# Pacing the weight-split loads of an adaLN transformer block by TensorE, storing the split weights one tile later, and the order of added exponential tiles

## The chip, the cores and the metric

The kernel runs on one core of a Trainium2 chip. The metric is the device time of one execution in microseconds, median over runs. TensorE (PE) does the matmuls, VectorE (DVE), ScalarE (ACT) and GpSimd (POOL) the elementwise work, and every DMA of this kernel is issued from one queue, that of SyncE (SP), which issues in its written order: an entry that has to wait holds all behind it.

## The reference

One transformer block on x of 2048 × 576 with 32 heads of 18 and an MLP of 4608, all in float32:

```python
mod = (silu(c) @ w_mod).reshape(1, 6, 1, 576)   # sa, ca, ga, sb, cb, gb
h = layernorm(x) * (1 + ca) + sa
x = x + ga * attention(h, wqkv, wo)             # softmax(q k^T / sqrt(18)) v, then wo
h = layernorm(x) * (1 + cb) + sb
x = x + gb * (silu(h @ w1) @ w2)
```

## The kernel before

Matmul operands are split into a high and a low float32r part, and a product is made of three matmuls (high × high, high × low, low × high). Weights arrive as plain float32. A weight tile is split once, on GpSimd, stored to a scratch tensor in HBM (`w1s`, `w2s`, `wos`), and later loaded from there as a pair, once for each of the four blocks of 512 query rows.

The work runs in stages:

1. A start (to about 155 us of the profile): layer norm, transposes, the first Q and K columns, V.
2. Attention, as a long row of slots: 32 heads in quads of 4, 4 query blocks, 32 slots to each quad and block. A slot holds two score matmuls in one orientation for the row maximum (`psa`, L727, reduced by VectorE at L729), two in the other (`psb`, L777) whose exponential ScalarE writes to a tile `pt` (L779), and the value matmuls (`psv`, L814) follow a few slots behind.
3. Beside the slots runs a *filler*, a list of pieces of other matmul work that a planner mixes in: first the remaining Q and K projections (`psqk`, L569, to about 612 us), then, for each query block that attention has finished, the output projection (`psp`), layer norm, and the MLP (`ps`, L483 and L477, one pair of w1 tiles after another, four w2 tiles at a time). The last block's MLP has no attention beside it (from about 2200 us).

TensorE's order is that of the program, set by the planner's modelled times. The other engines' order, SP's among them, is set when the kernel is built by a scheduler that simulates it: an instruction is placed when its inputs and buffers are free in that simulation, so a load that depends on nothing but a free buffer is placed early, whatever the place in the program it was asked for.

Names that the change and the prediction touch:

- `early` (L633) and `weights` (L636): split one weight tile of the filler's first stage. The list `splits` holds 36 tiles of w1 and 5 of wo; `add_qk` (L608) puts one after the second and one after the fourth quarter of each Q/K block of 14 matmuls. `weights` loads the raw tile in two halves (`raw`, L644, a ring of 3), makes the high part (L647) and the low part (L648) on GpSimd, and stores the pair (L649). A `we` tile has 2 buffers. In block 0 the 36 tiles of w2 go the same way (`w2_load`, L996), with a product by `gb` (L646) first. With `first` false it only loads the stored pair (L639).
- `load_k` (L689, DMA at L696): K tiles `ka` and `kb`, one chunk of 512 keys ahead; `load_quad` (L673): Q tiles `qt`; `load_v` (L700): `vt`; `max_rows` (L752): the row maxima go to HBM (`mscr`, L754) and back into two rows of `qt` (L758), and the `psb` matmuls of that quad wait for them.
- `qk_store` (L586, DMAs at L594 and L596): stores a projected block to `qscr` or `kscr`.
- `pts`, the ring of exponential tiles: `slot_b` (L760) takes the first of the list and moves it to the end. There are 7 until the MLP's pool is opened (`open_mlp`, L848), which frees the first stage's memory and adds 3 in it.
- `prefetch` (L865): loads the wo pairs and x for a block.
- `after_pe` (L457) makes an instruction wait for the last `psb` matmul issued so far (`state["pe"]`, L777).

Of the kernel before, what the change touches and what calls it, by code (L numbers as in the profile page):

```python
# [9 lines left out]
F32 = mybir.dt.float32  # L10
# [8 lines left out]
P = 128  # L19
# [7 lines left out]
QB = 512  # L27
# [32 lines left out]
PB = 7, 10  # L60
# [30 lines left out]
def f(ap):  # L91
    return ap.bitcast(F32)
# [247 lines left out]
def tile_adaln_block(ctx: ExitStack, tc: tile.TileContext, x, wqkv, wo, w1, w2, c, wfirst, wcol, out):  # L340
    nc = tc.nc
# [115 lines left out]
    def after_pe(ins):  # L457
        if state["pe"] is not None:
            tc.add_manual_dep(ins.ins, state["pe"].ins.name, SYNC, reason="its turn by the plan")
# [45 lines left out]
    mp = {}  # L505
# [127 lines left out]
    def early(src, scr, gate=None):  # L633
        weights(mp["e"].tile([P, 2, 640], F32R, tag="w", name="we", bufs=2)[:, :, :src.shape[1]], src, scr, True, gate)

    def weights(w, src, scr, first, gate=None):  # L636

        if not first:
            nc.sync.dma_start(f(w), f(scr))  # L639
            return  # L640
        n = w.shape[2] // 2
        for cs in (slice(0, n), slice(n, 2 * n)):
            raw = mp.get("p", mp.get("e")).tile([P, 320], F32, tag="raw", name="raw", bufs=3)[:, :n]
            nc.sync.dma_start(raw, src[:, cs])  # L644
            if gate is not None:
                nc.gpsimd.tensor_tensor(raw, raw, gate[:, cs], op=ALU.mult)  # L646
            nc.gpsimd.tensor_copy(w[:, 1, cs], raw)  # L647
            nc.gpsimd.tensor_tensor(w[:, 0, cs], raw, f(w[:, 1, cs]), op=ALU.subtract)  # L648
        nc.sync.dma_start(f(scr), f(w))  # L649

    steps = []
    for m in range(2, 4):
# [195 lines left out]
    def open_mlp():  # L848
        nonlocal psF, psA, psX
        psX = None  # L850
        fill.flush()
        rp.close()
        ps0.close()
        psF = ctx.enter_context(tc.tile_pool(name="psF2", bufs=2, space=PSUM))
        psA = ctx.enter_context(tc.tile_pool(name="psA2", bufs=3, space=PSUM))
        mp["p"] = ctx.enter_context(tc.tile_pool(name="mlp", bufs=1, side="right"))
        pts[:0] = [mp["p"].tile([P, 2, QB], F32, name=f"pt{i}") for i in range(*PB)]
        plan.ring("f", 2)
        plan.ring("b", 2)
        plan.ring("a", 3)  # L860
# [4 lines left out]
    def prefetch(b):  # L865
        pool = mp["p"]
        c = ready[b] = {}
        for kt in range(KT):
            if kt < 4:
                w = pool.tile([P, 2, KT * P], F32R, tag="w1", name="wo1", bufs=W1B)[:, :, :D]  # L870
            else:
                w = pool.tile([P, 2, D], F32R, tag="w2", name="wo2", bufs=5)
            weights(w, None, wos[kt], False)
            c["wo", kt] = w
        c["x1"] = []
        for j in range(NST):
            c["x1"].append(pool.tile([P, D], F32, name="x1", bufs=5))
            nc.sync.dma_start(c["x1"][j], x[b * QB + j * P:b * QB + (j + 1) * P, :])

    def post(b):  # L880
# [111 lines left out]
        def w_load(i):  # L992
            c["w1", i] = pool.tile([P, 2, KT * P], F32R, tag="w1", name="w1t", bufs=W1B)
            weights(c["w1", i], None, w1s[i], False)
# [463 lines left out]
    pts = [att.tile([P, 2, QB], F32, name=f"pt{i}") for i in range(PB[0])]  # L1458
# [31 lines left out]
    while now < 2 * (total + LEAD) or pend or later:  # L1490
        plan.advance()
        if "p" not in mp and fill.pos == len(fill.items):
            open_mlp()
            prefetch(0)
# [112 lines left out]
```

## Time and profile before

| | |
|---|---|
| median of 3 runs | 2491.09 us (2487.87 to 2494.18) |
| the profiled execution's own time | 2491.18 us |
| its span in the trace | 2489.4 us |
| TensorE matmul busy | 2357.8 us (95%) |
| VectorE busy | 1781.6 us (72%) |
| ScalarE busy | 1482.3 us (60%) |
| GpSimd busy | 627.6 us (25%) |
| DMA queue of SP, moved | 456.21 MB, 54.9% of 16 engines |
| mean granted TensorE clock | 0.975 of full |

A row such as "L777 PE MATMUL psb<-qt,kb ... x134 | 55.1, 514 | 49.9 <-DMA qt<-mscr 17.4" is a group: 134 instructions of line 777 that were busy for 55.1 us in all and 514 ns each, and the 49.9 us for which their engine stood idle just ahead of them, 17.4 of it until the DMA named. In a row of waits stand the us in total, the times and the longest. In the chain of waits stand the start, the us and the piece of work that the end of the kernel goes back to. "SPq" is the issuing queue of SP.

### The profile page before, as it was taken

What the parts mean: (1) busy time and instruction counts of PE and PEld (TensorE: products, weight loads), DVE (VectorE), ACT (ScalarE), POOL (GpSimd) and SP (SyncE); (2) the same over time, 40 slices, a digit from 0 to 9 for tenths busy, and PEclk for the clock granted to TensorE, in tenths of its full rate; (3) what the DMA queues carried; (4) which work ended last, traced back from release to release, by engine and by line L of the source; (5) the groups of instructions that cost most, each with busy time, mean ns of one, the idle gap of its engine ahead of it and who ended that gap; (6) DMA issues with size and microseconds to landing.
All of it is one profiled execution on the core that took longest, in us unless ns stands there. A gap on an engine that the chain in (4) does not pass through costs nothing.

```text
span 2489.4 us, 52376 instructions
## 1 busy us (share of the span) xinstructions
PE 2357.8 (95%) x19952; PEld 1615.3 (65%) x19952; DVE 1781.6 (72%) x3110; ACT 1482.3 (60%) x2736; POOL 627.6 (25%) x763
## 2 busy tenths in 40 slices
PE   6995789999899999999999999999999999989999
PEld 4862334443467777776667667776676777678988
DVE  7873568887688878888888778888887778234333
ACT  4243457776567766767577677766677667732121
POOL 5225531310433444444221111112211111120000
PEclk9996889999899999999999999999999999999999
DMA  7778874655544565556454554444654454326463
GB/s 249 245 223 272 275 236 150 185 185 168 173 161 158 188 206 175 178 193 199 159 187 161 193 179 166 173 157 160 208 180 158 159 179 166 130 103 237 171 220 119
DMA packets 208003, 459.56 MB, mean 185 GB/s; under 512 B 32010, under 2 KB 68266, under 8 KB 207754
## 3 DMA queue, kind: packets, MB, share of 16 engines
q1 hardware_dynamic: 207754, 456.21, 54.9%
q8 instruction: 160, 2.62, 0.4%
q14 instruction: 89, 0.73, 0.1%
HBM read 365.07 MB, written 86.33 MB: 181 GB/s over the span
## 4 chain that ended last, share of the span: by engine, by line
PE 82%; DMA 6%; DVE 5%; ACT 3%; POOL 2%; issue 2%; SPq 1%; ACTq 0%; POOLq 0%; DVEq 0%
PE ps L483 25%; PE psv L814 17%; PE psa L727 12%; PE ps L477 10%; PE psb L777 9%; PE psqk L569 3%; DMA raw<-in_w 3%; DVE mx L729 2%; PE psv L483 2%; PE psp L483 1%; DMA kb<-kscr 1%; PE psv L1262 1%; PE psqk L483 1%; ACT pt L779 1%; PE psqk L1262 1%
## 5 line engine op out<-in xcount | busy, mean ns | idle before, releaser
L729 DVE TENSOR_REDUCE mx<-psa 128x1 f32<-128x512 f32 x2048 | 1320.7, 684 | 367.9 <-PE psb L777 206.1
L779 ACT ACTIVATE pt<-psb 128x512 f32<-128x512 f32 x2048 | 1131.4, 598 | 554.2 <-PE psb L777 372.0
L777 PE MATMUL psb<-qt,kb 56*128 56x512 f32 x2048 | 762.3, 432 | 71.5 <-ACT pt L779 22.2
L727 PE MATMUL psa<-ka,qt 54*128 54x512 f32 x2016 | 703.8, 421 | 10.3 <-DVE mx L729 8.8
L727 PEld LDWEIGHTS psa<-ka,qt 54*128 54x128 f32 x2016 | 338.9, 189 | 308.3 <-DVE mx L729 205.8
L814 PE MATMUL psv<-pt,vt 128*32 128x512 f32 x4096 | 520.4, 612 | 1.0 <-ACT ov L818 0.9
L777 PEld LDWEIGHTS psb<-qt,kb 56*128 56x128 f32 x2048 | 357.1, 188 | 122.2 <-ACT pt L779 57.5
L483 PE MATMUL ps<-w2t,g 64*128 64x288 f32 x4992 | 408.5, 293 | 0.2
L483 PEld LDWEIGHTS ps<-w2t,g 64*128 64x128 f32 x4992 | 382.6, 186 | 30.7 <-DVE mx L729 7.5
L483 PE MATMUL ps<-hh,w1t 64*128 64x512 f32 x2160 | 397.9, 393 | 2.5 <-DVE x L920 1.5
L483 PEld LDWEIGHTS ps<-hh,w1t 64*128 64x128 f32 x2160 | 247.3, 185 | 37.9 <-DVE mx L729 7.5
L1040 POOL TENSOR_TENSOR g<-etmp,g 128x512 fp32r<-128x512 f32 x108 | 137.5, 1295 | 466.5 <-ACT g L1039 363.2
L814 PEld LDWEIGHTS psv<-pt,vt 128*32 128x32 f32 x4096 | 99.8, 109 | 216.7 <-issue 211.0
L924 POOL TENSOR_TENSOR x<-x,gt 128x288 f32<-128x288 f32 x116 | 93.2, 803 | 515.6 <-ACT gt L923 508.7
L483 PE MATMUL ps<-hl,w1t 64*128 64x512 f32 x864 | 200.2, 391 | 0.0
L920 DVE TENSOR_TENSOR x<-ps,x 128x288 f32<-128x288 f32 x184 | 83.8, 455 | 120.1 <-PE ps L477 76.6
L477 PE MATMUL ps<-w2t,g 128*128 128x288 f32 x960 | 133.0, 299 | 7.4 <-ACT g L1039 5.9
L477 PEld LDWEIGHTS ps<-w2t,g 128*128 128x128 f32 x960 | 130.6, 191 | 9.9 <-ACT g L1039 6.3
L483 PEld LDWEIGHTS ps<-hl,w1t 64*128 64x128 f32 x864 | 107.3, 186 | 9.3
L1036 ACT ACTIVATE eq<-ps 128x512 f32<-128x512 f32 x36 | 21.6, 600 | 146.3 <-PE ps L477 146.3
L477 PE MATMUL ps<-hh,w1t 128*128 128x512 f32 x360 | 106.9, 390 | 0.5 <-DVE hh L414 0.5
L1037 DVE SCALAR_TENSOR_TENSOR etmp<-etmp 128x512 f32<-128x512 f32 x108 | 76.2, 739 | 29.5 <-ACT etmp L1036 29.1
(139 smaller groups left out, 2022.6 us busy)
## 6 DMA issues: line engine op xcount, KB each, us to landing
w1t<-w1s SPq DMA_DIRECT2D x144, 640.0 KB
w2t<-w2s SPq DMA_DIRECT2D x108, 576.0 KB
kb<-kscr SPq DMA_DIRECT2D x512, 108.0 KB
ka<-kscr SPq DMA_DIRECT2D x504, 108.0 KB
w1s<-we SPq DMA_DIRECT2D x36, 640.0 KB
w2s<-w2t SPq DMA_DIRECT2D x36, 576.0 KB
vt<-vscr SPq DMA_DIRECT2D x32, 608.0 KB
qt<-qscr SPq DMA_DIRECT2D x128, 108.0 KB
```

The source lines that it names most:

```text
L477: mm(self.ps[late], lhsT=lhsT, rhs=rhs, start=(i == 0), stop=(i == self.n - 1))
L483: done = mm(self.ps[g], lhsT=lhsT[rows], rhs=rhs[rows], start=(s == 0), stop=(s == 2 * self.n - 1))
L569: mm(qk_ps[0], lhsT=w[b][:, kt, :], rhs=(hTl if a else hTh)[:, kt, n * 512:(n + 1) * 512], start=(i == 0), stop=(i == 13))
L727: mm(ps, lhsT=t["q"][64 * j:64 * j + 54, hp, stt * P:(stt + 1) * P], rhs=t["a" if ("a", kc, hp) in t else "b", kc, hp][64 * j:64 * j + 54, ...
L729: return lambda: nc.vector.tensor_reduce(t["mx"][:, 2 * j + hp, stt, kc:kc + 1], ps, axis=AX.X, op=ALU.max)
L777: state["pe"] = mm(ps, lhsT=t["b", kt // 4, hp][64 * e:64 * e + 56, kt % 4 * P:(kt % 4 + 1) * P], rhs=t["q"][64 * e:64 * e + 56, hp, :], s ...
L779: nc.scalar.activation(t["P"][kt, hp][:, e, :], ps, AF.Exp, scale=SCALE)
L814: mm(t["ps"][32 * h:32 * h + 32, :], lhsT=t["v"][:, c0:c0 + 32], rhs=t["P"][kt, h // 2][:, h % 2, :], start=(kt == 0), stop=(kt == NKT - 1 ...
L920: nc.vector.tensor_add(c["x1"][j][:, hs], ps, c["x1"][j][:, hs])
L924: nc.gpsimd.tensor_add(c["x1"][j][:, hs], c["x1"][j][:, hs], t)
L1037: nc.vector.scalar_tensor_tensor(t, t, 1.0, u, op0=ALU.add, op1=ALU.mult)
L1040: (nc.vector if last else nc.gpsimd).tensor_tensor(g[:, 1, :], t, f(g[:, 0, :]), op=ALU.subtract)
```

## The change

Three edits. The raw loads in `weights` wait, by `after_pe`, for the last `psb` matmul ahead of their place in the program. The store of a split tile is put off: it is noted in a list and issued at the beginning of the next call of `weights` (of either kind), it too after TensorE. The three added exponential tiles go to the end of the ring in place of its front. Lines from 636 on move: L644 becomes L652, L646 to L648 become L654 to L656, L649 becomes L641, L639 becomes L647, and what stands behind is 8 lines further down.

```diff
+    stores = []
+
+    def store_rest():
+        while stores:
+            w, scr = stores.pop()
+            after_pe(nc.sync.dma_start(f(scr), f(w)))
+
     def weights(w, src, scr, first, gate=None):
 
+        store_rest()
         if not first:
             nc.sync.dma_start(f(w), f(scr))
             return
         n = w.shape[2] // 2
         for cs in (slice(0, n), slice(n, 2 * n)):
             raw = mp.get("p", mp.get("e")).tile([P, 320], F32, tag="raw", name="raw", bufs=3)[:, :n]
-            nc.sync.dma_start(raw, src[:, cs])
+            after_pe(nc.sync.dma_start(raw, src[:, cs]))
...
-        nc.sync.dma_start(f(scr), f(w))
+        stores.append((w, scr))
...
-        pts[:0] = [mp["p"].tile([P, 2, QB], F32, name=f"pt{i}") for i in range(*PB)]
+        pts[:] = pts + [mp["p"].tile([P, 2, QB], F32, name=f"pt{i}") for i in range(*PB)]
```

TensorE's matmuls keep their order; of their operands only the exponential tiles' names change, from the opening of the MLP's pool on. What moves stands on SP. Its queue where attention and the Q/K filler begin, before (`raw`, `we`, `w1s` are the split of w1; `ka`, `kb`, `vt` attention's K and V):

```order
L703 DMA vt1_2100<-vscr_102 128x1216
L644 DMA raw_2270<-in_w1 128x320
L649 DMA w1s_103<-we_2149 128x1280
L644 DMA raw_2387<-in_w1 128x320
L696 DMA ka2_82<-kscr_100 54x512
L644 DMA raw_2391<-in_w1 128x320
L649 DMA w1s_103<-we_2265 128x1280
L696 DMA ka2_82<-kscr_100 54x512
L644 DMA raw_2525<-in_w1 128x320
L644 DMA raw_2529<-in_w1 128x320
L649 DMA w1s_103<-we_2386 128x1280
```

and now, from the same load of V on:

```order
L711 DMA vt1_2100<-vscr_102 128x1216
L652 DMA raw_2150<-in_w1 128x320
L652 DMA raw_2154<-in_w1 128x320
L704 DMA ka2_82<-kscr_100 54x512 x2
L704 DMA kb0_84<-kscr_100 54x512 x2
L704 DMA ka3_83<-kscr_100 54x512
L704 DMA kb1_85<-kscr_100 54x512
L704 DMA ka3_83<-kscr_100 54x512
L704 DMA kb1_85<-kscr_100 54x512
L641 DMA w1s_103<-we_2149 128x1280
L652 DMA raw_2266<-in_w1 128x320
L652 DMA raw_2270<-in_w1 128x320
```

Before, three w1 tiles are stored in the time of one K tile; now eight K loads stand between the first tile's raw loads and its store.

ScalarE at the opening of the MLP's pool, before (L573 and L580 are the last Q/K block's copies, `pt7` to `pt9` the new tiles):

```order
L779 ACTIVATE pt0_2092<-psb_6942 128x512
L580 ACTIVATE qkhl_6948<-psqk_6795 128x512
L573 ACTIVATE qt_6950<-psqk_6795 128x512
L779 ACTIVATE pt7_6971<-psb_6995 128x512
L779 ACTIVATE pt7_6971<-psb_7001 128x512
L779 ACTIVATE pt8_6972<-psb_7012 128x512
```

and now:

```order
L787 ACTIVATE pt0_2092<-psb_6941 128x512
L580 ACTIVATE qkhl_6947<-psqk_6794 128x512
L573 ACTIVATE qt_6949<-psqk_6794 128x512
L787 ACTIVATE pt1_2093<-psb_6995 128x512
L787 ACTIVATE pt1_2093<-psb_7001 128x512
L787 ACTIVATE pt2_2094<-psb_7012 128x512
```

The first exponentials behind the opening go to tiles of the old ring; `pt7` comes after `pt1` to `pt6` and `pt0`.

SP behind the opening, before (`wo2` and `x1` are block 0's projection weights and rows of x):

```order
L639 DMA wo2_6982<-wos_105 128x1152
L878 DMA x1_6984<-in_x 128x576
L878 DMA x1_6986<-in_x 128x576
L878 DMA x1_6988<-in_x 128x576
L878 DMA x1_6990<-in_x 128x576
L644 DMA raw_7884<-in_w2 128x288
L644 DMA raw_7889<-in_w2 128x288
L644 DMA raw_8302<-in_w2 128x288
L878 DMA x1_15397<-in_x 128x576
L696 DMA ka2_82<-kscr_100 54x512 x2
L696 DMA kb0_84<-kscr_100 54x512 x2
L644 DMA raw_8307<-in_w2 128x288
```

and now:

```order
L647 DMA wo2_6982<-wos_105 128x1152
L886 DMA x1_6984<-in_x 128x576
L886 DMA x1_6986<-in_x 128x576
L886 DMA x1_6988<-in_x 128x576
L886 DMA x1_6990<-in_x 128x576
L704 DMA ka2_82<-kscr_100 54x512 x2
L886 DMA x1_15397<-in_x 128x576
L704 DMA kb0_84<-kscr_100 54x512 x2
L704 DMA ka3_83<-kscr_100 54x512 x2
L704 DMA kb1_85<-kscr_100 54x512 x2
```

The raw loads of w2 have left this place; the first now stands behind the first two loads of w1 pairs, at the beginning of block 0's MLP.

## The prediction

> **What bounds the kernel now.** I first read the busy time by stretch, because the mean over the span (TensorE 95% busy) hides stages. The stretches are cut where the work changes: 155 us is where attention starts beside the Q/K projections, 612 us where these end, 680 us where the MLP of block 0 begins. Columns: stretch and its length, then busy us (instructions) of TensorE, its weight loads, VectorE, ScalarE, GpSimd, then granted clock, DMA share, GB/s.
>
> ```profile
> core 0: us, PE busy (x) PEld busy (x) DVE busy (x) ACT busy (x) POOL busy (x), PEclk, DMA share, GB/s
> 155.00:180.00 25.00, 24.54 (x141) 10.52 (x144) 21.90 (x36) 17.33 (x33) 12.04 (x21) 1.00 0.78 250
> 180.00:335.00 155.00, 103.40 (x490) 43.30 (x483) 68.39 (x115) 62.71 (x119) 85.50 (x127) 0.77 0.82 272
> 335.00:400.00 65.00, 62.44 (x362) 26.20 (x362) 53.40 (x91) 45.55 (x89) 12.98 (x13) 0.97 0.63 201
> 400.00:600.00 200.00, 199.21 (x1216) 84.26 (x1215) 172.64 (x296) 151.97 (x297) 41.16 (x46) 1.00 0.54 171
> ...
> 612.00:672.00 60.00, 46.37 (x203) 17.79 (x203) 34.37 (x59) 31.47 (x58) 22.77 (x31) 0.76 0.66 220
> 680.00:1185.00 505.00, 494.21 (x4734) 349.39 (x4734) 411.67 (x696) 349.39 (x644) 213.06 (x275) 0.99 0.55 182
> 1185.00:1690.00 505.00, 500.41 (x4950) 359.00 (x4951) 407.65 (x699) 350.18 (x643) 88.15 (x90) 1.00 0.51 171
> ```
>
> From 400 us on TensorE is the bound: idle under 1% in 400–600, about 5 us in the whole of block 1 (1185–1690). Two holes stand ahead of that: 180–335 (51.6 us idle, and the granted clock down to 0.77, so the busy part is slow too) and 612–672 (13.6 us idle, 0.76). A hole's size must therefore be measured in work, not in idle time. The groups by line give the work, for 155–335 and then for 400–600:
>
> ```profile
> L777 PE MATMUL psb<-qt,kb 56*128 56x512 f32 x134 | 55.1, 514 | 49.9 <-DMA qt<-mscr 17.4 <-DMA kb<-kscr 14.9 <-issue 9.8
> ```
> ```profile
> L777 PE MATMUL psb<-qt,kb 56*128 56x512 f32 x255 | 89.3, 441 | 0.3 <-ACT pt L779 0.2
> ...
> L569 PE MATMUL psqk<-hTh,wql 128*128 128x512 f32 x63 | 26.1, 415 | 0.0
> L569 PE MATMUL psqk<-hTh,wqh 128*128 128x512 f32 x63 | 26.0, 413 | 0.0
> L569 PE MATMUL psqk<-hTl,wqh 128*128 128x512 f32 x50 | 21.8, 436 | 0.0
> ```
>
> At full pace a score matmul into psb, with all that goes round it, comes every 200/255 = 0.784 us. The 134 of 155–335 are worth 105 us; they took 180. TensorE waits there for K and Q tiles, that is, for transfers that stand late on SP's queue. The chain of waits says behind what:
>
> ```profile
> 179.92 4.78 DMA raw<-in_w
> 184.76 0.88 POOL we L647 x2
> 185.64 1.65 POOL we L648 x2
> 187.31 0.32 SPq L649
> 187.68 3.59 DMA raw<-in_w
> 191.31 0.08 issue
> 191.39 0.45 POOL we L647
> ...
> 242.03 0.89 PE psb L777 x2
> ```
>
> It is a loop of its own: raw load, two splits on GpSimd, the store that waits for them on SP, the next raw load. Between 180 and 242 us no work of TensorE is on the chain. The waits of SP and GpSimd in 155–335, and how many instructions of the loop ran there, agree:
>
> ```profile
> SPq L644 <- POOL we L648: 31.2, 20, 2.6
> SPq L644 <- DMA raw<-in_w: 10.7, 9, 2.7
> SPq L649 <- POOL we L648: 9.0, 16, 2.0
> ```
> ```profile
> POOL we L647 <- DMA raw<-in_w: 78.9, 48, 6.8
> ```
> ```profile
> L644 SPq DMA_DIRECT2D raw<-in_w x70: 327/382/1402, 157.7 to 332.8; - x70
> L647 POOL CAST we<-raw x69: 442/453/465, 162.3 to 334.0; 128x320 fp32r<-128x320 f32 x69
> L648 POOL TENSOR_TENSOR we<-raw,we x68: 854/867/887, 164.0 to 332.8; 128x320 fp32r<-128x320 f32 x68
> ```
>
> So about 34 of the 36 w1 tiles are split in this one burst, though the program asks for one after every half Q/K block; SP is in order, and the K, Q and max-row transfers of attention stand between.
>
> **The change, part by part.** (1) *Raw loads wait for TensorE.* No work is added or removed: the same 82 early raw loads and 41 stores, the same splits (0.45 + 0.87 us each). They are spread. A Q/K block is 14 matmuls; 176 in 400–600 are 12.6 blocks, so 25 splits per 200 us, one per 8.0 us, and 41 splits need 326 us of full pace: 155 to about 480 instead of 155 to 340. GpSimd's share of a tile, 2 × 1.32 = 2.6 us, lies inside those 8 us, and so does a raw load (up to 4.8 us) before it. Queued behind a waiting raw load on SP are K, Q and V loads; they are wanted by later score matmuls than the one waited for, and mostly wait for TensorE to free their buffer anyway, so I cost the wait itself at nothing; if that cover fails it is rival C.
>
> What the cover can't hide is the DMA. In 155–335 its engines were busy 25 × 0.78 + 155 × 0.82 = 147 us; the attention and Q/K work done then needs 105 × 0.54 = 57 (pace of 400–600). The remaining 90 us over some 33 tiles are 2.7 us a tile, 0.34 of each 8.0 us. Spread, the DMA is wanted at 0.54 + 0.34 = 0.88. No longer stretch shows more than 0.82, so as an estimate the 326 us become 326 × 0.88/0.82 = 350: 24 us given back (0 if the engines can run at 0.88, since SP was blocked in the burst; all 75 if 0.82 came with starvation as its price). I take 24, by the nearest row. Part 1: 180 − 105 = 75, plus the 335–400 tail (65 us for 76 score matmuls, by the row below worth 60: 5 us), less 24: **−56**.
>
> ```profile
> L777 PE MATMUL psb<-qt,kb 56*128 56x512 f32 x76 | 28.3, 455 | 1.8 <-DMA kb<-kscr 1.6
> ```
>
> (2) *Stores one tile later.* Of SP's 51 us above 40 are waits of a raw load (for its buffer) or of a store for GpSimd. A tile later GpSimd has been done for some 2 us (8.0 − 4.8 − 2.6, less a Q/K subtraction in between), so the store passes. This is needed for part 1 and adds nothing to its sum; if it were late, SP would stand 1 to 2.6 us a tile as now.
>
> (3) *New exponential tiles last.* At 612 us ScalarE's next exponential goes into a new tile whose memory held old buffers, and waits for a store of Q to land:
>
> ```profile
> ACT pt L779 <- DMA qscr<-qkhl: 5.6, 1, 5.6
> ```
> ```profile
> 611.58 4.01 DMA qscr<-qkhl
> ...
> 617.70 1.93 PE psv L814 x8
> ...
> 622.29 1.92 PE psv L814 x8
> ...
> 631.23 0.99 PE psv L814 x8
> ...
> 634.36 1.00 PE psv L814 x8
> ```
>
> Then TensorE needs 13.5 us for three rounds (from one group of eight value matmuls to the next, 617.70 to 631.23) where a later round takes 3.13: about 5 us of standing and 4.1 of slow clock. With an old tile next, free since long, both go; a new tile comes seven tiles later, some 10 us on, when the store (4 us) has landed. **−9**; bounds 0 and −10.
>
> The slow rounds bear on every short stall. The Trainium skill's page "TensorE: Matmul & The Clock Gate" (Part 1) says that an idle window of about 3.4 us drops the array to half clock until a busy one has passed. The groups of 1.93 against 0.99 us agree with the half; by its window alone each stall would cost some 3.4 us of half-speed work, as an estimate, where the rows here show 12 us of it.
>
> (4) *The w2 loads of block 0 leave the opening.* Eleven raw loads of w2 (and four stores) were issued between these two rows of SP's timeline, ahead of max rows and V:
>
> ```profile
> 622.28 4.10 SPq L644 DMA_DIRECT2D raw<-in_w  x3
> ...
> 653.77 0.42 SPq L644 DMA_DIRECT2D raw<-in_w  x1
> ```
>
> Of 612–672, 13 rounds (50 score matmuls) at 3.13 would be 41 us; 60 were used. Past part 3, 10 us remain; I take 4, as the output-projection and x loads stay ahead of attention's.
>
> (5) *w2 through block 0.* 680–1185 has 10.8 us idle against 4.6 in the next block: at best −6. At worst raw loads that start late hold GpSimd, with the low halves of g behind them; now it already waits often, off the path:
>
> ```profile
> POOL raw L646 <- DMA raw<-in_w: 71.5, 41, 5.4
> ```
>
> I take −2, within −6 and +15 (three tiles late by 5.4).
>
> Sum: −56 − 9 − 4 − 2 = −71. The profiled execution took 2491.2 us (span 2489.4), 0.1 over the median. **2420 us**.
>
> **The rivals.** *A, all of it comes back:* the DMA runs at 0.88 without stalls: 2491 − 80 − 10 − 6 = 2395. For it: SP stood for 51 of 180 us, when it could feed the DMA nothing, and 0.82 came out all the same. Against it: K loads then meet a nearly full DMA. *B, the DMA keeps the hole open:* it is bytes, not order; raw and store traffic at 0.88 delays K loads, each stall trails slow clock, and a third of part 1 remains: 2491 − 25 − 9 = 2457. For it: 0.82 and starvation stand in the same row. *C, slower:* a raw load waits on SP for TensorE while K or Q loads behind it are already due, so TensorE waits for its own follower. Price: 77 tiles (41 early, 36 of w2); the seven kb waits of the burst averaged 14.9/7 = 2.1 us (first row below). It cancels the 71 from 0.92 us a tile; at 2.1 on two thirds of them it is +108: 2528. Against it: in 400–600 SP waits for TensorE at K loads too (second row), and that stretch runs full.
>
> ```profile
> PE psb L777 <- DMA kb<-kscr: 14.9, 7, 6.1
> ```
> ```profile
> SPq L696 <- PE psa L727: 37.5, 28, 3.8
> ```
>
> *D, nothing:* early issue was worth as much as the burst costs, or the paced loads come too late for GpSimd: 36 w2 tiles late by 5.4 us, a third of it reaching TensorE, is +65, and 2485 remains, within noise. Beside it stands the Trainium skill's page "DMA: Bandwidth & Descriptors" (rules for kernel authors): issue a DMA early and wait for it late. By that rule this change errs. The trace so far bears out the opposite in 155–335, where the loads that went early were those not wanted for hundreds of us.
>
> **How the numbers follow.** Forecast 0.57 (own range 2403 to 2440: DMA loss 7 to 42), A 0.13, B 0.15, C 0.10, D 0.05. Within 0.3% (7.5 us, about what runs of this kernel can't tell from no change) is D: 0.05. Slower is C: 0.10; faster the rest, 0.85. The range reaches to A and just past B, 2390 to 2462.
>
> **What would show it.** Right: in the stretch of the burst psb matmuls every 0.8 to 0.85 us and clock near 1.0; raw loads spread evenly to about 500 us; DMA share 0.8 or more throughout; SP's waits for GpSimd at raw loads and stores nearly gone, waits for psb in their place; no wait of an exponential for the Q store; the Q/K work over near 612 - 56 = 556 us. Wrong: kb waits of TensorE summing to tens of us in 155–480 (B), or SP waits of raw loads for psb ending just before late K loads (C).

## The result and the profile after

The changed kernel takes 2490.34 us (2483.98 to 2500.11, 12 runs), the kernel before 2491.06 us (2487.57 to 2494.18, 12 runs): a ratio of 1.0, 95% interval 0.9987 to 1.0013. Forecast were 2420 us and a gain. The profiled execution took 2487.03 us (span 2485.2).

The time is the same, yet the kernel runs quite differently. First the same stretches of the changed kernel as were shown of the one before (stretch, its length, busy us and instructions of TensorE, its weight loads, VectorE, ScalarE, GpSimd, then granted clock, DMA share, GB/s):

```profile
155.00:180.00 25.00, 24.77 (x139) 10.79 (x142) 20.53 (x34) 17.18 (x33) 6.53 (x11) 0.93 0.63 206
180.00:335.00 155.00, 144.20 (x832) 60.69 (x828) 119.64 (x198) 104.58 (x199) 60.87 (x83) 0.97 0.74 244
335.00:400.00 65.00, 61.83 (x362) 26.23 (x358) 51.40 (x88) 45.26 (x90) 26.12 (x36) 0.95 0.77 243
400.00:600.00 200.00, 184.19 (x1081) 75.75 (x1073) 157.73 (x268) 137.37 (x265) 59.71 (x79) 0.96 0.68 222
...
680.00:1185.00 505.00, 477.54 (x4363) 334.43 (x4359) 375.40 (x610) 322.67 (x596) 217.04 (x279) 0.95 0.55 177
1185.00:1690.00 505.00, 500.50 (x4926) 360.32 (x4928) 405.24 (x695) 349.42 (x641) 86.46 (x88) 0.99 0.51 171
```

The first hole is closed: in 180–335 TensorE runs 832 matmuls instead of 490, idle for 10.8 us instead of 51.6, at a clock of 0.97 instead of 0.77. But 680–1185, the MLP of block 0, which was full before (10.8 us idle, clock 0.99), now has 27.5 us idle and 0.95. It holds 371 matmuls fewer; at that stretch's former pace of 505/4734 = 0.107 us each, they are worth 40 us.

The groups of 155–335 in the changed kernel, and the raw tile's issues in 155–640 (count, shortest, median and longest ns, first and last start):

```profile
L785 PE MATMUL psb<-qt,kb 56*128 56x512 f32 x206 | 76.5, 456 | 7.0 <-DMA qt<-mscr 4.9 <-DMA kb<-kscr 1.9
```
```profile
L652 SPq DMA_DIRECT2D raw<-in_w x72: 327/424/1920, 159.5 to 470.0; - x72
```

206 score matmuls stand where 134 stood, and the raw loads of w1 are spread to 470 us. So the pacing did what it says.

Where the gain went is seen by counting work. ScalarE's exponentials are in the same order in every one of these kernels, so the start of the nth, counted from zero, is a milestone. The table, worked out from the starts in one trace of each kernel, has the lead of each kernel over the one before at such a milestone (minus: earlier; the last column is the last exponential, with only the MLP of block 3 behind it). It serves for the experiments too.

| kernel | 64 | 192 | 448 | 544 | 800 | 1056 | last |
|---|---|---|---|---|---|---|---|
| before: start, us | 242.8 | 384.0 | 586.4 | 693.2 | 953.1 | 1207.9 | 2198.4 |
| the change | −38 | −61 | −40 | −54 | −36 | −4 | −4 |
| e1_w2_free | −34 | −58 | −40 | −47 | −52 | −52 | −53 |
| e2_ring_alone | −1 | −2 | −2 | −14 | −16 | −17 | −15 |
| e3_w2_alone | 0 | 0 | 0 | −12 | +17 | +47 | +49 |
| e4_store_at_once | −36 | −57 | −33 | −50 | −15 | +30 | +31 |
| e5_raw_free | −33 | −46 | −24 | −34 | −39 | −33 | −33 |
| e6_raws_first | −36 | −60 | −42 | −57 | −41 | −20 | −20 |
| e7_w2_raw_free | −38 | −63 | −40 | −50 | −56 | −55 | −55 |
| e8_store_twice | −38 | −48 | −4 | −13 | −15 | −13 | −13 |
| e9_w2_asked_earlier | −36 | −59 | −41 | −54 | −47 | −35 | −34 |
| e10_spread_48 | −34 | −66 | −53 | −53 | −61 | −60 | −60 |
| e11_earlier_raws_first | −35 | −59 | −38 | −51 | −49 | −34 | −34 |

The changed kernel is 61 us ahead at exponential 192, loses 21 while the split goes on, regains 14 at the opening of the MLP's pool, and is 54 ahead at 544. Between 544 and 1056, the MLP of block 0, it gives back 50. Behind that nothing moves.

What TensorE, GpSimd and SP wait for in 680–1185 of the changed kernel (engine and line, whom for: us in total, times, longest):

```profile
PE ps L483 <- POOL w2t L655: 15.2, 9, 2.3
PE ps L483 <- POOL w2t L656: 7.4, 16, 0.7
```
```profile
POOL raw L654 <- DMA raw<-in_w: 162.0, 39, 11.0
```
```profile
SPq L641 <- POOL w2t L656: 64.2, 26, 5.2
SPq L704 <- PE psb L785: 56.8, 43, 5.6
SPq L704 <- PE psa L735: 53.6, 37, 6.4
SPq L652 <- POOL w2t L656: 44.4, 10, 8.6
```

The second matmul of the MLP (L483) stands for the split w2 tile: 22.6 us in 25 waits. GpSimd's wait for raw tiles has grown from 71.5 to 162.0 us. One group of four w2 tiles shows how. SP's timeline of the changed kernel around the loads of its third and fourth tile (start, us, what, count):

```profile
750.15 0.32 SPq L641 DMA_DIRECT2D w2s<-w2t  x1
750.51 1.61 SPq L652 DMA_DIRECT2D raw<-in_w  x3
...
764.42 0.37 SPq L652 DMA_DIRECT2D raw<-in_w  x1
```

The same on GpSimd and on TensorE (in brackets the idle time ahead, and what ended it):

```profile
759.32 3.21 POOL L654 TENSOR_TENSOR raw<-raw,gb 128x288 f32<-128x288 f32 x3 [6.70 <-DMA raw<-in_w]
762.47 1.17 POOL L655 CAST w2t<-raw 128x288 fp32r<-128x288 f32 x3
763.60 2.29 POOL L656 TENSOR_TENSOR w2t<-raw,w2t 128x288 fp32r<-128x288 f32 x3
```
```profile
760.08 0.97 PE L483 MATMUL ps<-w2t,g 64*128 64x288 f32 x12
...
762.95 0.77 PE L483 MATMUL ps<-w2t,g 64*128 64x288 f32 x2 [1.35 <-POOL w2t L655]
...
767.98 0.61 PE L483 MATMUL ps<-w2t,g 64*128 64x288 f32 x2 [1.93 <-POOL w2t L655]
```

Four half tiles go through three raw buffers: three loads leave at 750.5, are there at 759.3, and the fourth can leave only at 764.4, when GpSimd has given a buffer back. The group's first matmul starts at 760.08, so TensorE reaches the third and fourth tile before GpSimd has made them. In the kernel before the same two tiles were asked for like this, and used like this:

```profile
701.61 0.42 SPq L644 DMA_DIRECT2D raw<-in_w  x1
783.19 0.37 SPq L644 DMA_DIRECT2D raw<-in_w  x1
784.39 0.34 SPq L644 DMA_DIRECT2D raw<-in_w  x1
785.93 0.36 SPq L644 DMA_DIRECT2D raw<-in_w  x1
```
```profile
810.75 0.96 PE L483 MATMUL ps<-w2t,g 64*128 64x288 f32 x12
```

The last half left 25 us ahead of the first matmul, instead of 4 us behind it. Block 0's 36 w2 tiles pass in nine groups of four. In the second to the eighth, by the starts in the traces, the last half left 22 to 25 us ahead of the group's first matmul in the kernel before, and leaves between 2.6 us ahead of it and 4.3 behind it now. From a group's first such matmul to its last TensorE takes 236 us in all nine together before and 282 now, so 46 of the 50 us lie there. That the late loads are the cause is so far a reading; the experiments test it.

### The profile page after: what moved, and what is told of

It reads as the page before. It is cut to its first block, busy times and chain, and to the rows that moved or that the text cites. A ratio compares the mean times of both kernels' runs of the same rounds, so it can differ in the third digit from the quotient of the medians.

```text
span 2485.2 us, 52362 instructions
## 1 busy us (share of the span) xinstructions
PE 2369.4 (95%) x19952; PEld 1625.0 (65%) x19952; DVE 1785.8 (72%) x3110; ACT 1483.6 (60%) x2736; POOL 631.1 (25%) x763
## 4 chain that ended last, share of the span: by engine, by line
PE 79%; DMA 7%; DVE 5%; POOL 3%; ACT 2%; issue 2%; SPq 1%; POOLq 0%; ACTq 0%; DVEq 0%
PE ps L483 24%; PE psv L822 16%; PE psa L735 12%; PE ps L477 10%; PE psb L785 8%; DMA raw<-in_w 4%; PE psqk L569 3%; DVE mx L737 2%; PE psv L483 2%; PE psp L483 1%; DMA kb<-kscr 1%; POOL raw L654 1%; PE psqk L483 1%; POOL w2t L655 1%; POOL w2t L656 1%
## 5 line engine op out<-in xcount | busy, mean ns | idle before, releaser
L483 PE MATMUL ps<-w2t,g 64*128 64x288 f32 x4992 | 428.6, 299 | 26.0 <-POOL w2t L655 15.2
L483 PEld LDWEIGHTS ps<-w2t,g 64*128 64x128 f32 x4992 | 395.2, 190 | 65.5 <-POOL w2t L655 18.6
L483 PE MATMUL ps<-hh,w1t 64*128 64x512 f32 x2160 | 397.3, 393 | 1.8 <-DVE x L928 1.5
L483 PEld LDWEIGHTS ps<-hh,w1t 64*128 64x128 f32 x2160 | 246.5, 185 | 36.8 <-DVE mx L737 7.5
L483 PE MATMUL ps<-hl,w1t 64*128 64x512 f32 x864 | 199.5, 391 | 0.0
L483 PEld LDWEIGHTS ps<-hl,w1t 64*128 64x128 f32 x864 | 107.1, 186 | 9.1
L654 POOL TENSOR_TENSOR raw<-raw,gb 128x288 f32<-128x288 f32 x72 | 61.5, 868 | 164.1 <-DMA raw<-in_w 164.1
```

Source lines behind the costliest of these rows:

```text
L483: done = mm(self.ps[g], lhsT=lhsT[rows], rhs=rhs[rows], start=(s == 0), stop=(s == 2 * self.n - 1))
```

## The experiments

The kernels ran in three sets (e1 to e4, e5 to e8, e9 to e11), each beside runs of the kernel before, with medians of 2494.35, 2492.84 and 2488.99 us; each ratio is to those of its own set.

**e1_w2_free.** The change, but block 0's w2 as before: its raw loads not tied to TensorE, its stores at once.

```diff
-            after_pe(nc.sync.dma_start(raw, src[:, cs]))
+            ld = nc.sync.dma_start(raw, src[:, cs])
+            if "p" not in mp:
+                after_pe(ld)
...
-        stores.append((w, scr))
+        if "p" in mp:
+            nc.sync.dma_start(f(scr), f(w))
+        else:
+            stores.append((w, scr))
```

> The change, but the w2 loads and stores of block 0 as before it (not paced, stored at once). Theory W (the early gain is real, and pacing w2 gives it back in block 0): the lead of 53 us that the changed kernel has at exponential 544 stays, plus the 4 us that it kept: 2491 - 53 = 2438, within 2430 to 2450; TensorE waits for no w2 split in block 0. Rival M (block 0's pace is set by something else that the early stage feeds, the w1 pairs or the DMA, and takes the lead whatever w2 does): 2480 to 2492.

Measured: 2442.79 us, ratio 0.9796 (0.9776 to 0.9816), within theory W's range. The lead of 47 at exponential 544 stays (−52 at 1056). Block 0 in this kernel:

```profile
680.00:1185.00 505.00, 500.30 (x4902) 355.57 (x4903) 412.40 (x696) 352.39 (x652) 207.61 (x268) 1.00 0.56 182
```

TensorE is idle for 4.7 us of 505. The loss belongs to the w2 part, and nothing else of the change makes block 0 slow.

**e2_ring_alone.** The kernel before with one line of the change, the ring's.

```diff
-        pts[:0] = [mp["p"].tile([P, 2, QB], F32, name=f"pt{i}") for i in range(*PB)]
+        pts[:] = pts + [mp["p"].tile([P, 2, QB], F32, name=f"pt{i}") for i in range(*PB)]
```

> The kernel before with the order of the added exponential tiles alone changed. Theory R (the wait of 5.6 us and the slow clock behind it go): 2491 - 8 = 2483, ratio 0.9964 to 0.998. Rival: the next stall, the V load at 660 us, takes it up: 2491, ratio 0.999 to 1.001.

Measured: 2479.33 us, 0.9944 (0.9928 to 0.996). All of the lead appears between exponentials 448 and 544 (−2 to −14). The chain of waits, at the place where before three rounds took 13.5 us:

```profile
612.98 1.00 PE psv L814 x8
616.10 1.00 PE psv L814 x8
619.23 1.00 PE psv L814 x8
622.36 1.00 PE psv L814 x8
625.49 1.00 PE psv L814 x8
```

The rounds go straight through, 3.13 us apart, at full clock. The theory of part 3 of the prediction holds; the gain, 12 us at this place and 14 by the ratio, is larger than the 8 expected here and lies past the range.

**e3_w2_alone.** The kernel before with the change's pacing and put-off stores for block 0's w2 alone (old ring, w1 and wo as before). The lines are against the change, and the ring's line goes back too.

```diff
+            if "p" in mp:
+                after_pe(ld)
...
+        if "p" not in mp:
+            nc.sync.dma_start(f(scr), f(w))
+        else:
+            stores.append((w, scr))
```

> The kernel before with only the w2 loads of block 0 paced and their stores put off; early stage and ring as before. Theory W: block 0 loses what it loses in the changed kernel, some 45 us, less some 5 us that leave the opening: 2491 + 40 = 2531, within 2520 to 2540. Rival M: 2485 to 2495.

Measured: 2538.15 us, 1.0178 (1.0159 to 1.0198). This part alone, on a kernel that is not early at anything, makes it 44 us slower, and between exponentials 544 and 1056 it loses 60 (−12 to +47), where 45 were expected. By the starts between, 52 of these come behind exponential 576, where the groups of w2 begin; ahead of it TensorE waits once for 9.5 us, for VectorE. The edit also brings 12 us at the opening, without the ring's edit: the raw loads of w2 that stood there have gone. The ring's gain comes first (e2 has −12 at exponential 496, e3 −3), that of the leaving loads behind it, and yet they don't add up: with both, the change gains 14 there. Why is not shown. Block 0, and TensorE's waits in it:

```profile
680.00:1185.00 505.00, 466.92 (x4224) 326.81 (x4222) 368.48 (x612) 314.32 (x579) 208.24 (x265) 0.94 0.54 173
```
```profile
PE ps L483 <- POOL w2t L657: 18.1, 12, 2.1
PE ps L483 <- POOL w2t L658: 7.1, 16, 0.7
```

The same waits as in the change. Undone, the loss is gone (e1); done alone, it is there (e3).

**e4_store_at_once.** The change with every split tile stored at once; raw loads paced as in the change.

```diff
-        stores.append((w, scr))
+        nc.sync.dma_start(f(scr), f(w))
```

> The change with the stores issued at once, as before it; raw loads paced, ring changed. Theory S (the store one tile later is needed: SP else stands for the raw load's landing and 2.6 us of GpSimd at each tile, with K loads behind it): 20 to 40 us lost in the early stage, 2510 to 2530. Rival: K loads have slack for it, 2485 to 2495; in block 0, where the next call comes at once, both expect no difference.

Measured: 2523.44 us, 1.0124 (1.0101 to 1.0147). The total is within what one theory expected, but not at the place that it named: its trace ends 34 us behind the change's, and of these only 7 are lost by exponential 448. In block 0, where both theories expected no difference, 80 are given back instead of 50. SP's waits there:

```profile
SPq L657 <- POOL w2t L656: 86.8, 28, 8.0
...
SPq L652 <- POOL w2t L656: 41.5, 8, 7.9
```

The store now stands directly behind the split that it waits for, and holds the next tile's raw load: 86.8 us at the store (L657) where the change had 64.2 (L641). TensorE's waits for the split tiles rise from 22.6 to 39.0 us in this trace. Putting the store off is worth most where the loads are late already.

**e5_raw_free.** The change with raw loads not paced anywhere, stores put off and paced.

```diff
-            after_pe(nc.sync.dma_start(raw, src[:, cs]))
+            nc.sync.dma_start(raw, src[:, cs])
```

> The change without its first edit: raw loads are not paced, the stores still come one tile later behind TensorE, the ring is as changed. Theory G (the paced stores alone pace the early stage, since a split tile has two buffers and the third split waits for the first store; raw loads may then run ahead by a tile or two, which block 0 needs): the early lead of 45 to 55 us is kept and block 0 loses nothing, 2430 to 2445. Rival P (it is the pace of the raw loads that ends the burst; without it only the ring's gain is left): 2475 to 2485.

Measured: 2451.02 us, 0.9831 (0.9802 to 0.9859): past one theory's range by 6, and far from the rival's. The lead at 448 is 24 instead of 40, at the end 33; but the trace is of an execution of 2459.03 us, 8 above the median, so how much smaller the early lead is in most executions is not shown. In block 0 nothing is lost (−34 to −33). So the paced stores alone pace much of the first stage: a split tile has two buffers, and a third can't be split before a store has left. That this is how they do it is read from the code, and wasn't tried by itself.

**e6_raws_first.** The change with the next tile's paced raw loads put on SP ahead of the previous tile's store.

```diff
-        store_rest()
         if not first:
+            store_rest()
             nc.sync.dma_start(f(w), f(scr))
...
+        halves = []
         for cs in (slice(0, n), slice(n, 2 * n)):
...
+            halves.append((cs, raw))
+        store_rest()
+        for cs, raw in halves:
```

> The change with the next tile's raw loads ahead of the store of the last one, all of them paced. Theory H (block 0 loses because SP stands at the store for GpSimd before it may issue the next tile's raw loads, so that load, split and store go one after the other, some 8.7 us a tile): the loss of 50 us in block 0 falls to 10 to 20, 2445 to 2465. Rival K (the raw loads are asked for too late in any order, as they wait for TensorE's place): no more than 10 us better, 2480 to 2492.

Measured: 2471.07 us, 0.991 (0.9895 to 0.9924), between the two theories. Block 0 gives back 37 instead of 50, and TensorE's waits there fall from 22.6 to 16.2 us:

```profile
PE ps L483 <- POOL w2t L659: 11.8, 6, 2.7
PE ps L483 <- POOL w2t L660: 4.4, 12, 0.6
```

The store ahead of the loads is a part of the lateness, and not the larger one.

**e7_w2_raw_free.** The change with only the raw loads of w2 freed; its stores stay put off and paced.

```diff
-            after_pe(nc.sync.dma_start(raw, src[:, cs]))
+            ld = nc.sync.dma_start(raw, src[:, cs])
+            if "p" not in mp:
+                after_pe(ld)
```

> The change with the w2 raw loads of block 0 not paced, their stores still one tile later and paced; beside the run in which both were as before (2443). Theory: the raw loads' pace alone makes the loss, the stores are of no account: 2438 to 2448. Rival: half of the loss is the paced stores', 2455 to 2475.

Measured: 2439.31 us, 0.9792 (0.9754 to 0.9829); nothing is given back (−50 at 544, −55 at 1056). With e1 this settles which half of the w2 edit costs: the raw loads' tie, alone. Stores put off cost nothing once the loads are early.

**e8_store_twice.** e1 with a second store of each early split tile to a spare tensor: more bytes in the first stage, the same waits and order.

```diff
+    spare = dram.tile([P, 2, KT * P], F32R, name="spare")
...
             after_pe(nc.sync.dma_start(f(scr), f(w)))
+            if "p" not in mp:
+                after_pe(nc.sync.dma_start(f(spare[:, :, :w.shape[2]]), f(w)))
```

> The kernel that ran at 2443 (change, w2 of block 0 as before), with each early split tile stored a second time, to a spare tensor that nothing reads: 41 stores and some 26 MB more. Theory D (the DMA's load is what gives back some 20 us of the lead between exponentials 192 and 448): the same again or more, 2465 to 2500. Rival L (what is given back is order and latency, not load): 2440 to 2455.

Measured: 2482.51 us, 0.9967 (0.9955 to 0.9979), as theory D expected. The lead shrinks from 48 to 4 between exponentials 192 and 448, where e1's goes from 58 to 40. Its stretches, and TensorE's waits in 155–600:

```profile
180.00:335.00 155.00, 133.37 (x761) 56.37 (x753) 108.28 (x183) 95.55 (x182) 53.76 (x74) 0.92 0.82 287
335.00:400.00 65.00, 59.21 (x321) 25.87 (x323) 44.07 (x77) 41.20 (x81) 26.11 (x34) 0.92 0.91 317
```
```profile
PE psb L793 <- DMA kb<-kscr: 24.7, 10, 7.7
```

Spreading doesn't make the transfers free: bytes that are put in their way cost time, as K loads that come late: TensorE's waits for them are 24.7 us, in e1 9.8. Since an entry on SP came with each, this doesn't part the bytes from the issue.

**e9_w2_asked_earlier.** The change, with w2 tiles two to four of a group put earlier in the filler's list, in block 0's second to eighth group of nine; still paced. `(k, i)` stands for the load of tile i ahead of piece k of that pair's first matmul.

```diff
-                add_mlp1(i0 + 2, [(NG // 2, i0 + 1)])
-                add_mlp1(i0 + CH, [(0, i0 + 2), (0, i0 + 3)])
+                early2 = b == 0 and i0 > 0
+                add_mlp1(i0 + 2, [(1, i0 + 1), (NG // 2, i0 + 2), (NG - 2, i0 + 3)] if early2 else [(NG // 2, i0 + 1)])
+                add_mlp1(i0 + CH, [] if early2 else [(0, i0 + 2), (0, i0 + 3)])
```

> The change with the second to fourth w2 tile of each group of four (from the second group on) asked for up to one MLP pair earlier in the program; still paced, order of raw loads and stores as in the change. Theory C (the chain of load, split and store, 8.7 us a tile and 35 us for four, is what is late; the tiles already follow one another without a pause): no more than 10 us better than the change, 2480 to 2492. Rival K (the place in the program is what is late): 2445 to 2460.

Measured: 2454.49 us, 0.9864 (0.9846 to 0.9882). My own theory, that the chain of load, split and buffer is too slow however early it is asked, fell; the rival held. Every load is still tied to TensorE, every wait is still there, and by the ratio 34 us have come back by the place alone. TensorE's waits for split tiles in 680–1185:

```profile
PE ps L483 <- POOL w2t L655: 1.7, 1, 1.7
PE ps L483 <- POOL w2t L656: 0.9, 2, 0.5
```

From 22.6 to 2.6 us. The table still shows 19 lost between 544 and 1056. The starts at milestones between say where: 9 by exponential 672, in the first two groups, of which the first was not moved, nothing from there to 992, and 10 from 992 to 1056. There the last group is loaded, which this edit doesn't move either, and the chain of waits runs through its raw loads and splits from 1119.5 to 1146 us, and then through a load of V that SP issued behind them. So most of the 19 stands at groups that were left as they were; whether moving them too would bring it back was not tried.

**e11_earlier_raws_first.** e9 and e6 together (both edits stand above).

> Both: the w2 tiles asked for earlier, and the next tile's raw loads ahead of the last one's store; all still paced. If chain and place both count, as the 20 us of the order alone suggest, a tile then costs GpSimd's 4.2 us and the loss in block 0 is nearly gone: 2440 to 2455. If pace itself is what costs (any wait for TensorE at a w2 raw load is too late): 2465 or more, no better than the order alone (2471).

Measured: 2448.35 us, 0.984 (0.9819 to 0.986). That is within the range for chain and place both, and the other theory, that any pace is too late, fell. But the interval overlaps e9's, and the trace is of an execution of 2457.97 us, well above the median, so whether the order of store and loads adds anything once the place is early is not shown.

**e10_spread_48.** e7, with the 41 early tiles spread over 48 places of the Q/K work: every seventh is skipped.

```diff
                     if p % 2 == 1 and splits:
-                        fill.add(0, splits.pop(0))
+                        turns[0] += 1
+                        if turns[0] % 7:
+                            fill.add(0, splits.pop(0))
```

> The kernel that ran at 2439 (w2 raw loads not paced) with the 41 early tiles spread over all 48 places of the Q/K work, every seventh left out. Theory D (the DMA's load gives back 20 us of the early lead, and twice the stores give back 40 more): one seventh less load for its time gives 3 to 8 us, 2431 to 2437. Rival: what is given back is set by latency at single places, no difference, 2437 to 2442.

Measured: 2430.32 us, 0.9757 (0.9739 to 0.9776), the fastest median of all, just past the range expected; its interval overlaps e7's. In the trace the lead at 448 is 53 instead of 40, and the stretch of the former hole is full:

```profile
180.00:335.00 155.00, 149.30 (x880) 64.29 (x880) 125.41 (x210) 111.14 (x212) 60.70 (x80) 0.99 0.73 244
```

5.7 us idle at a clock of 0.99. But the 13 us don't last: at exponential 544 the lead is 53, where the change has 54 and e7 50. The step that makes the change a gain is thus to leave w2's raw loads alone (e7); whether spreading the early tiles wider adds to it is not shown.

## Why the prediction was wrong

**The step that failed is part 5**, "w2 through block 0": −2 us was taken, "within −6 and +15 (three tiles late by 5.4)". Measured was a loss of 50 us (the table, 544 to 1056), and of 52 behind exponential 576 in e3, with this part alone. The prediction had the mechanism in a clause, "raw loads that start late hold GpSimd", and set it aside with the row of GpSimd's waits: "now it already waits often, off the path". That row told of the kernel before, where a wait of GpSimd for a raw tile cost nothing since the tile was asked for 25 us ahead of its use. Tied to TensorE, the same load leaves, in the group shown, some 10 us ahead (750.5 to 760.1), and needs 8.8 us to land (750.5 to 759.3) and 4.4 to be split (three halves took 3.21 + 1.17 + 2.29 us on GpSimd, a tile has two), 13.2 us in all, with only three buffers for the four halves of two tiles. In the six groups that follow, the third tile's load leaves 7 to 13 us ahead and takes 3.3 to 7.4 to reach GpSimd; there it is above all the last half, held back by the three buffers, that is late. The slack had been the cover, and the edit took it away. The question that the prediction asked at w1, when is this wanted and how long does it take, was not asked at w2. The bound was mis-sized too: three late tiles, where TensorE stood idle in each of the nine groups.

**The rival D** named it: paced loads that come too late for GpSimd, 36 tiles × 5.4 us × 1/3 = 65, a total of 2485, chance 0.05. What came is its mechanism and nearly its size (50 given back). The rule that stood beside it, from the Trainium skill's page "DMA: Bandwidth & Descriptors" (rules for kernel authors), to issue early and wait late, holds in block 0 by e3 and e9 (52 us lost by late loads, 34 regained by early ones); in the first stage the runs show the opposite, where loads issued early held up others and pacing them and their stores gained 61 us by exponential 192. One rule, and both signs in one kernel: what parts them is when the load is wanted.

**Part 1** was right in mechanism: the hole closed, SP's 51 us at raw loads and stores in 155–335, spent on GpSimd and on loads, fell to 11.9 (the sum of the three rows below), and score matmuls came every 180/206 = 0.87 us against 0.80 to 0.85 expected. In size it was 16 too large: −56 predicted, −40 at exponential 448, and the last Q/K matmul at 569 us instead of 609, where 556 was expected. Its give-back for the DMA, 24 us, compares with 21 between 192 and 448; but the prediction lets it run from 155 us on, so how the 16 are parted between it and the 80 us that were to come first is not shown. e8 shows that the give-back grows with traffic, and e10 that a slower pace only puts 13 of it off. The prediction let it come from a DMA share of at most 0.82; e8 held 0.91 for 65 us, so that ceiling was none, and K loads come late at shares below it.

```profile
SPq L641 <- POOL we L656: 7.5, 4, 2.3
...
SPq L652 <- POOL we L656: 2.5, 2, 1.8
...
SPq L652 <- DMA raw<-in_w: 1.9, 1, 1.9
```

**Part 2**, zero and needed: zero was right for the sum, needed was not. By e4 the put-off stores bring 7 us by exponential 448, so that 33 of the 40 come without them, and 30 in block 0, where the prediction didn't look. Its working also has a slip: 8.0 − 4.8 − 2.6 is 0.6 us and not some 2.

**Parts 3 and 4**, −9 and −4: together −13 predicted, −14 measured. But e2 shows the ring bringing 12 alone and e3 the leaving loads 12 alone. The two terms don't add as the prediction added them, and that their sum came out is luck.

The miss is 70 us, and 67 in the profiled execution, which the table counts: 52 are part 5 and 16 part 1, less 1 in parts 3 and 4.

**The rivals** A (all of it comes back) and B (K loads keep a third of the hole) did not come as such: TensorE's waits for K in 155–600 sum to 9.9 us, in five waits:

```profile
PE psb L785 <- DMA kb<-kscr: 9.9, 5, 4.1
```

C, TensorE waiting for its own follower, did not come in the first stage; in e5, with raw loads free, the early stage was not better (16 us worse in its one trace).

## What to carry to other kernels

To tie a load to the progress of the engine that will use it, compare two times at each place: from the place it is asked for to the first use, and from issue through landing, splitting and the return of its buffer. Pace what isn't wanted for long (61 us gained here), and leave free, or ask for earlier, what is wanted within that second time (50 lost). A wait that costs nothing in the profile of before costs nothing only as long as its slack is there, and an edit that moves the load moves the slack.

## What the runs showed of the hardware

The DMA engines were busy for 0.91 of a stretch of 65 us, at 317 GB/s (e8), higher than in any of the stretches read before, while the work beside them slowed: 321 matmuls, where e1, without the second stores, has 348 at a share of 0.79. And short stalls go with a lower clock: in 680–1185 of the change TensorE was never idle for more than 2.3 us at a time, and the granted clock was 0.95, against 1.00 in e1, where the stretch is full. Of the 40 us that the count of matmuls there is short by, 16.7 are added idle time. The larger share passed while TensorE was busy: 477.54 us for 4363 matmuls are 109 ns each, where 494.21 for 4734 are 104 before, 5% more at a clock 4% lower. That the stalls lower the clock was not tried by itself.
